# Top-k attention into a Fourier mixing block: the token folds of batches 1 to 6 at one piece a step without a pause, with two fold buffers that change roles for the second parity, and three places for the transposed attention output

## The chip, the core and the metric

The kernel runs on one NeuronCore of a Trainium2 chip. A core has five engines that each work through their own list of instructions in order: TensorE (PE in the profile, with its weight loads as PEld), VectorE (DVE), ScalarE (ACT), GpSimd (POOL) and SyncE (SP, which here only issues DMA transfers). They meet at semaphores. The metric is the device time of one execution in microseconds (us).[...]

## The reference: what is computed

The inputs are q, k and v of shape (8, 8, 576, 64): 8 batches, 8 heads, 576 tokens, 64 channels, and two weights of shapes (512, 2048) and (2048, 512). Everything is float32.

```python
scores = scale * np.matmul(q, k.transpose(0, 1, 3, 2))
kth = np.partition(scores, -32, axis=-1)[..., -32:-31]
scores = np.where(scores >= kth, scores, -1e9)
attn = softmax(scores)                       # over the keys
x = (attn @ v).transpose(0, 2, 1, 3).reshape(8, 576, 512)
mixed = np.real(np.fft.fft(np.fft.fft(x, axis=1), axis=2))
u = x + mixed
un = (u - mean(u)) / sqrt(var(u) + 1e-6)     # over the 512 channels
out = u + np.maximum(un @ w_ch1, 0) @ w_ch2
```

(`softmax` stands for the lines that subtract the largest score, take the exponential and divide by the sum.) The attention of a batch must be complete, for all heads and tokens, before its Fourier part can begin, since that part sums over tokens and over channels.

## The kernel before, in words

**Steps and items.** Two heads make a pair, and a batch has four pairs. A pair's 576 query rows are worked through as nine items: four blocks of 128 rows for each of two heads, and one item that holds the last rows of both. That gives 288 items, 36 to a batch. The program is written by one loop over steps `i`; in each it emits, for all engines, the scores of item `i + 3` (TensorE, lines 368 and 398), the top-32 search of item `i` (VectorE, four MAX8 and three MATCH_REPLACE8 of 576 columns, lines 422 and 424), the threshold `nt` (GpSimd, line 431), mask and exponential of the items just before (ScalarE 445 and 456, GpSimd 448), and the transposition of the probabilities, on TensorE (lines 524 to 539) or, for most pairs, by DMA through a table in DRAM (`planes`, lines 482 and 503). `attend` (line 561) multiplies the probabilities by v, for a pair in two chunks of query columns. `attended` copies the result to a tile `xT` (line 575), and `to_tokens` later transposes it (line 601), multiplies by the reciprocal sums and writes `x`, the batch's 576 by 512 tile. A list `pending` says which chunks are between the two; a chunk of batch b is held there while batch b - 2 has not been stored, as there are two `x` tiles.

**The Fourier part.** The transform over tokens uses symmetry. `fold_ops` makes, for each parity of the frequency (`par` 0 and 1), four pieces: `first` adds or subtracts the two halves of the tokens (`sd`, line 716), `second` adds and subtracts the two halves of the channels (`zw`, line 675), `both` and the last piece fold the channels further (`fg`, lines 648 to 671). For batches 1 to 6 GpSimd does this. `dft_tokens` (line 752) then multiplies `fg` by a table on TensorE, `dft_channels` (lines 809 and 813) does the transform over channels, the result is copied (ScalarE 830), added to `x` (GpSimd 836), normalised by statistics on VectorE (`stats`, lines 841 and 842; `rsqrt`) and transposed (`channels_first`, lines 878 and 881).

**The buffers of the fold.** `sd` takes the buffer `fold_s`, `zw` takes `fold_d`, and `fg` takes `fold_s` again. Both parities use them the same way, so that the second parity's `sd` may only be written when TensorE has read the first parity's `fg`. The two buffers also hold other things at other times, among them the tail's fold, the copy `us`, the transposed `unT` and the MLP's sums `ct`.

**The plan.** Work around the top-k stream is put at fixed steps by `at(step, place, function, cost)`. Batch b's last item is `end`, and its Fourier part begins at `T0`, which is `end + 3` for batch 1, `end + 5` for batches 2 to 6 and `end + 4` for the last. `ft` holds the steps of the two `dft_tokens`, `fc` the first step of `dft_channels`. `arrivals` holds the step at which a batch's MLP is handed to a queue.

**The queue.** The MLP of a batch is cut into units of TensorE work: `hidden` (line 963) and the products of the second layer (lines 990, 1029 and 1160; the latter are the seven products of a scheme with fewer multiplications). A unit has a cost in microseconds written beside it. At each arrival `level` chooses the smallest even load a step, up to about 6.4, at which the queue is empty by the next arrival, and `some` takes units out of the queue between the step's fixed TensorE work until the load is reached. Units that are not done by then stay in the queue ahead of the next batch's. After the last item there is no more top-k work, and TensorE does what is in the queue, then the last batch's Fourier part and MLP. The weights of the seven products are brought from DRAM by `bring` (line 906), on SyncE's queue.

Of the kernel before, what the change touches and what calls it, by code (L numbers as in the profile page):

```python
# [9 lines left out]
F32 = mybir.dt.float32  # L10
# [9 lines left out]
P = 128  # L20
# [53 lines left out]
def kernel(  # L74
# [9 lines left out]
    nc = tc.nc  # L84
    B, H, S, D = q.shape
# [17 lines left out]
    CW = (2 * P + TAIL, 2 * P)  # L103
# [11 lines left out]
    attp = ctx.enter_context(tc.tile_pool(name="attp", bufs=2))  # L115
# [454 lines left out]
    def attended(pair, ch, late):  # L570

        o, w = o_of.pop((pair, ch)), CW[ch]
        PT.pop((pair, ch))
        xT = attp.tile([P, CW[0]], F32, name=f"xT_{pair}_{ch}", tag="xT", bufs=4)
        nc.scalar.copy(out=xT[:, 0:w], in_=o[:, 0:w])
        xT_of[pair, ch] = xT
        den = den_t[pair % 3]
        if ch == 0:
            for h in range(2):
                nc.scalar.copy(  # L580
                    out=den[TH * h:TH * (h + 1), 5:6],
                    in_=den[TAIL + TH * h:TAIL + TH * (h + 1), 4:5],
                )
        c0, n = (0, 6) if ch == 0 else (6, 4)
        rd = small.tile([P, 6], F32, name=f"rd_{pair}_{ch}", tag="rd", bufs=6)

        nc.scalar.activation(out=rd[:, 0:n], in_=den[:, c0:c0 + n], func=AF.Copy, bias=1e-9)
        late.append(lambda: nc.vector.reciprocal(out=rd[:, 0:n], in_=rd[:, 0:n]))
        rd_of[pair, ch] = rd
# [83 lines left out]
    def fold_halves(eng, s_, z):  # L673
        for cols, op in ((slice(0, Q2), ALU.add), (slice(Q2, DM), ALU.subtract)):
            eng.tensor_tensor(out=z[..., cols], in0=s_[..., 0:Q2], in1=s_[..., Q2:DM], op=op)
# [20 lines left out]
    def fold_ops(b, par, eng, space="own"):  # L696

        x = x_of[b]  # L700

        if space == "hT":
            sp = batp.tile([P, NIT * CW[0]], F32, name=f"fsp_{b}", tag="hT")

        def buf(n, name, cols=DM):
            if space == "hT":
                return sp[:, 2 * DM * n:2 * DM * n + 2 * cols].rearrange("p (s c) -> p s c", s=2)
            pool, tag = (batp, ("fold_s", "fold_d")) if space == "own" else (attp, ("PT0", "PT1"))
            return pool.tile([P, 2, cols], F32, name=f"{name}_{b}_{par}", tag=tag[n % 2], bufs=1)

        got = folded[b, par] = []

        def first():
            got.append(buf(0, "sd"))
            op = ALU.add if par == 0 else ALU.subtract
            eng.tensor_tensor(out=got[0], in0=x[:, 0:2, :], in1=x[:, 2:4, :], op=op)

        def second():
            got.append(buf(1, "zw"))
            fold_halves(eng, got[0], got[1])  # L720

        def third(n):
            if n == 0:
                got.append(buf(2, "fg", DM + Q2))
            fold_channels(eng, got[1], got[2][:, :, 0:DM], got[2][:, :, DM:DM + Q2], n)

        def both():
            third(0)
            third(1)

        return [first, second, both, lambda: third(2)]
# [565 lines left out]
    def at(step, where, fn, cost=0.0):  # L1297
        plan.setdefault((step, where), []).append(fn)
        costs[step] = costs.get(step, 0.0) + cost
# [75 lines left out]
    for b in range(B):  # L1375
        end = PER_BATCH * (b + 1) - 1
        last = b == B - 1
        first, soon = b == 0, b == 1
        T0 = end + (2 if first else 3 if soon else 4 if last else 5)
        if first:  # L1380

            for op in fold_tails(b, nc.gpsimd):
                at(T0 - 1, "pool", op)

            def folds(b=b):
                for par, space in ((0, "own"), (1, "hT")):
                    for op in fold_ops(b, par, nc.vector, space):
                        op()
            at(T0, "dve", folds)
            ft, fc = (T0 + 1, T0 + 1), T0 + 1  # L1390
        elif soon:

            for n, op in enumerate(fold_tails(b, nc.gpsimd)):
                at(T0 - 2 + n, "pool0", op)
            for par in range(2):
                def folds(par=par, b=b, T0=T0):
                    for n, op in enumerate(fold_ops(b, par, nc.gpsimd)):
                        at(T0 + 1 + 3 * par + min(n, 2), "pool0", op)
                at(T0, "begin", folds)
            ft, fc = (T0 + 4, T0 + 7), T0 + 8  # L1400
        elif not last:
            for n, op in enumerate(fold_tails(b, nc.gpsimd)):
                at(T0 - 2 + n, "pool0", op)
            for par in range(2):
                def folds(par=par, b=b, T0=T0):
                    for n, op in enumerate(fold_ops(b, par, nc.gpsimd)):
                        at(T0 + (6 if par else 1) + n, "pool0", op)
                at(T0, "begin", folds)
            ft, fc = (T0 + 5, T0 + 11), T0 + 12
        else:  # L1410
            for op in fold_tails(b, nc.gpsimd):
                at(T0 - 1, "pool0", op)

            def folds(b=b):
                for op in fold_ops(b, 0, nc.vector) + fold_ops(b, 1, nc.vector, "PT"):
                    op()
            at(T0, "dve", folds)

            at(T0 + 1, "pe1", lambda: one_unit() + one_unit() if len(queue) > 1 else 0.0)
            ft, fc = (T0 + 1, T0 + 3), T0 + 4  # L1420
        for par in range(2):
            at(ft[par], "pe1", lambda b=b, par=par: dft_tokens(b, par), 4.3)
        for n, t in enumerate((0, 1, 4, 2, 3)):
            quick = first or last
            s = fc + (0 if first else n // 3 if last else n // 2)
            at(s, "pe2", lambda b=b, t=t, q=quick: dft_channels(b, t, q), 1.75)
            if not quick:
                at(s, "pool2", lambda b=b, t=t: add_mixed(b, t))
                at(s + 1, "dve", lambda b=b, t=t: stats(b, t))
            at(s + (1 if quick else 2), "pe", lambda b=b, t=t: channels_first(b, t), 0.6)  # L1430
            if first and t == 4:
                at(s + 1, "pe", lambda: (queue.extend(waiting), waiting.clear()) and 0.0)
        at(s + 1, "begin" if quick else "dve", lambda b=b: rsqrt(b))
        arrivals.append(s + (1 if quick else 2))
        at(arrivals[-1], "units", lambda b=b: (queue if b else waiting).extend(mlp_units(b)))
# [51 lines left out]
    while i < N + 5 or plan or queue or sums:  # L1487
# [26 lines left out]
        if pending and pending[0][0] <= i and (  # L1514
            i < 2 * PER_BATCH + 4 or chunk_at(i)[0] is None
        ):
            _, pp, pc = pending[0]
# [12 lines left out]
        if short:  # L1530
            fixed += tok
            pair, r = divmod(i - 1, PER_PAIR)
# [39 lines left out]
        pair, ch = chunk_at(i)  # L1572
# [78 lines left out]
```

## Time and profile before

| | |
|---|---|
| median of three runs | 1882.73 us (1879.72 to 1884.17) |
| the profiled execution | 1882.96 us, of which the profile spans 1881.2 us |
| TensorE (PE) busy | 1713.1 us, 91% of the span |
| VectorE (DVE) busy | 1582.7 us, 84% |
| ScalarE (ACT) busy | 1295.7 us, 69% |
| GpSimd (POOL) busy | 911.3 us, 48% |
| mean granted TensorE clock | 0.955 of full speed |

How to read it: an engine's busy time is the sum over its instructions in one profiled execution. Busy shares are means over stages that have different limits, so that the stages have to be looked at one by one. A wait is put down to the instruction whose semaphore came last. The duration of a matmul is partly modelled, as matmuls are pipelined. In what follows "step i" in the trace is the moment at which GpSimd begins the threshold `nt` (line 431) of item i: step 39 is at 262.2 us, 88 at 541.6, 126 at 745.9, 162 at 954.9, 198 at 1167.6, 234 at 1370.7, 270 at 1575.9, and the last item, 287, at 1688.1.

### The profile page before, as it was taken

To read this page: it belongs to the slowest core of one execution; us is meant where nothing else is said; L and a number is where in the kernel's file an instruction comes from. 1 tells how busy PE (TensorE), PEld (TensorE's weight loads), DVE (VectorE), ACT (ScalarE), POOL (GpSimd) and SP (SyncE) were. 2 spreads that over 40 slices of the span, in tenths; PEclk is the share of its full clock that TensorE was granted. 3 is DMA by queue.
4 is the path that set the end of the run, shared out by engine and by line. 5 is a ranking of instruction groups with operands and counts; after the bars stand their busy time and mean duration, and the time that the engine had idled before them with its cause. 6 is when DMAs were issued, how large, how long until landed. Compare 5 with 4: busy or idle time off the path is not lost.

```text
span 1881.2 us, 26922 instructions
## 1 busy us (share of the span) xinstructions
PE 1713.1 (91%) x8134; PEld 1086.5 (58%) x8134; DVE 1582.7 (84%) x3301; ACT 1295.7 (69%) x3104; POOL 911.3 (48%) x1278
## 2 busy tenths in 40 slices
PE   5567699889899998989999999999999999999999
PEld 3344364364466654666456665666556655666677
DVE  7999999798899999998899998999999999862110
ACT  6878658576788778777777677777787678652100
POOL 4768643455645356354544465355544465341012
PEclk8887899899899999999999999999999999999999
DMA  5333026651468755585455854685466756440132
GB/s 167 105 96 109 24 60 171 175 138 51 118 155 212 178 125 129 149 214 131 123 144 151 215 128 121 141 229 147 125 155 180 179 133 143 121 117 6 51 110 72
DMA packets 516576, 249.16 MB, mean 132 GB/s; under 512 B 398288, under 2 KB 506448, under 8 KB 516432
## 3 DMA queue, kind: packets, MB, share of 16 engines
q1 hardware_dynamic: 515664, 247.23, 50.7%
q8 instruction: 65, 1.06, 0.2%
q14 instruction: 79, 0.65, 0.1%
q10 hardware_dynamic: 768, 0.21, 0.0%
HBM read 93.63 MB, written 84.74 MB: 95 GB/s over the span
## 4 chain that ended last, share of the span: by engine, by line
PE 66%; ACT 10%; DVE 9%; POOL 7%; issue 3%; DMA 3%; SPq 2%; POOLq 0%; DVEq 0%; ACTq 0%
PE hp L963 24%; PE cp L990 8%; PE o L561 7%; PE sp L398 5%; DVE m L422 4%; PE cw L1160 4%; DVE wk L424 4%; PE yp L752 3%; PE cv L1160 3%; PE cp L1029 3%; POOL wk L448 2%; ACT wk L469 2%; ACT wk L445 2%; PE sp_t L368 2%; ACT S L456 1%
## 5 line engine op out<-in xcount | busy, mean ns | idle before, releaser
L448 POOL TENSOR_TENSOR wk<-S,wk 128x576 f32<-128x576 f32 x288 | 406.7, 1412 | 532.5 <-ACT wk L445 509.8
L422 DVE MAX8 m<-wk 128x8 f32<-128x576 f32 x864 | 626.5, 749 | 6.1
L963 PE MATMUL hp<-unT,w 128*128 128x256 f32 (+1 forms) x2048 | 535.3, 412 | 3.8 <-ACT hT L967 2.6
L963 PEld LDWEIGHTS hp<-unT,w 128*128 128x128 f32 x2048 | 379.4, 192 | 134.5 <-issue 33.4
L424 DVE MATCH_REPLACE8 wk<-m,wk 128x576 f32<-128x576 f32 x576 | 427.4, 742 | 0.0
L469 ACT COPY wk<-S 128x576 uint16<-128x576 uint16 x468 | 288.7, 666 | 0.0
L445 ACT ACTIVATE wk<-S,nt 128x576 f32<-128x576 f32 x288 | 222.5, 773 | 92.6 <-POOL nt L431 91.8
L422 DVE MAX8 m<-S 128x8 f32<-128x576 f32 x288 | 213.9, 743 | 45.1 <-ACT S L372 45.1
L990 PE MATMUL cp<-w,hT 128*128 128x512 f32 x512 | 244.0, 613 | 0.0
L561 PE MATMUL o<-PT,v 128*64 128x256 f32 (+3 forms) x1440 | 203.9, 427 | 21.8 <-DMA PT<-planes 9.9
L967 ACT ACTIVATE hT<-hp 128x320 f32<-128x320 f32 (+1 forms) x256 | 103.4, 408 | 160.2 <-PE hp L963 159.2
L424 DVE MATCH_REPLACE8 wk<-m,S 128x576 f32<-128x576 f32 x288 | 213.5, 741 | 0.0
L456 ACT ACTIVATE S<-wk,nt 128x576 f32<-128x576 f32 x234 | 182.4, 780 | 38.3 <-POOL wk L448 37.3
L398 PE MATMUL sp<-kT,qT 64*128 64x512 f32 (+1 forms) x528 | 181.5, 684 | 12.2 <-ACT means L1348 5.1
L561 PEld LDWEIGHTS o<-PT,v 128*64 128x64 f32 x1440 | 117.0, 157 | 105.7 <-issue 33.8
L401 ACT COPY S<-sp 128x512 f32<-128x512 f32 (+1 forms) x264 | 141.5, 586 | 29.5 <-PE sp L398 28.2
L990 PEld LDWEIGHTS cp<-w,hT 128*128 128x128 f32 x512 | 92.9, 194 | 107.8 <-issue 106.0
L1105 POOL TENSOR_TENSOR hT<-hT 128x512 f32<-128x512 f32 x64 | 81.3, 1274 | 105.1 <-ACT hT L967 91.2
L431 POOL TENSOR_TENSOR nt<-m,cc 128x2 f32<-128x2 f32 x288 | 59.2, 206 | 140.3 <-DVE m L422 139.3
L368 PE MATMUL sp_t<-kt,qT 128*128 128x128 f32 x320 | 70.5, 303 | 43.3 <-ACT S L390 24.4
L368 PEld LDWEIGHTS sp_t<-kt,qT 128*128 128x128 f32 x320 | 55.2, 195 | 92.3 <-ACT S L390 32.4
L1160 PE MATMUL cw<-w,hT 128*128 128x256 f32 x448 | 105.9, 383 | 0.5 <-issue 0.4
(160 smaller groups left out, 2133.1 us busy)
## 6 DMA issues: line engine op xcount, KB each, us to landing
planes<-wk SPq DMA_DIRECT2D x208, 288.0 KB, 2.7
w<-w_parts SPq DMA_DIRECT2D x82, 512.0 KB, 4.7
space<-in_moe_w_ch_dram SPq DMA_DIRECT2D x32, 512.0 KB, 3.7
nat<-in_q_dram SPq DMA_DIRECT2D x128, 64.0 KB, 2.4
v<-in_v_dram SPq DMA_DIRECT2D x64, 128.0 KB, 2.9
out_dram<-x SPq DMA_DIRECT2D x32, 256.0 KB, 2.6
nat<-in_k_dram SPq DMA_DIRECT2D x62, 128.0 KB, 2.9
planes<-wk SPq DMA_DIRECT2D x52, 144.0 KB, 2.7
```

Source lines behind the costliest of these rows:

```text
L368: nc.tensor.matmul(sp[:, 0:P], lhsT=qT[:, q_end - P:q_end], rhs=kt_t, start=True, stop=True)
L398: nc.tensor.matmul(sp[r], lhsT=qT[hd, q_cols], rhs=kT[hd, :], start=True, stop=True)
L422: ops.append(lambda src=src, m8=m8: nc.vector.max(out=m8, in_=src))
L424: ops.append(lambda src=src, m8=m8: nc.vector.match_replace(w, m8, src, NEG))
L445: nc.scalar.activation(out=w, in_=Ssb[i], func=AF.Relu, scale=-FAR, bias=Nt[i][:, 1:2])
L448: nc.gpsimd.tensor_tensor(out=w, in0=Ssb[i], in1=w, op=ALU.subtract)
L456: nc.scalar.activation(out=Ssb[i] if by_dma(i) else w, in_=w, func=AF.Exp, bias=Nt.pop(i)[:, 0:1], accum_out=den_t[pair % 3][:, c:c + 1],)
L469: nc.scalar.copy(out=words[:, half, :], in_=src[:, half, :])
L561: nc.tensor.matmul(o[D * e:D * (e + 1), c0:c1], lhsT=vv[:, c, e, :], rhs=pt[:, NF if c == NF else (NF + 1) * e + c, c0:c1], start=(c == 0) ...
L963: nc.tensor.matmul(hp[:, 0:w], lhsT=w1[:, dt, P * it:P * (it + 1)], rhs=unT[:, dt, 0:w], start=(dt == 0), stop=(dt == NDT - 1),)
L990: nc.tensor.matmul(cp, lhsT=hT[:, it, P * n:P * (n + 1)], rhs=w2[:, it, :], start=(it == 0), stop=(it == NIT - 1),)
L1160: nc.tensor.matmul(dst, lhsT=h()[a][:, kc, :], rhs=rhs_of(kc), start=start and kc == 0, stop=kc == NK - 1, skip_group_check=True,)
```

## The change

Three things are altered.

- The rule for batch 1 and the rule for batches 2 to 6 become one. The four pieces of the first parity stand at steps `T0 + 1` to `T0 + 4`, those of the second at `T0 + 5` to `T0 + 8`, one a step. `dft_tokens` stands at `T0 + 5` and `T0 + 9`, and `dft_channels` begins at `T0 + 10`. Before, batch 1 had two pieces in one step, with `fc` at `T0 + 8`; batches 2 to 6 had a step without a piece between the parities, with `fc` at `T0 + 12`.
- For batches 1 to 6 the second parity uses the two fold buffers the other way round: `sd` in `fold_d`, `zw` in `fold_s`, `fg` in `fold_d`.
- `xT` has three places instead of four.

```diff
-        xT = attp.tile([P, CW[0]], F32, name=f"xT_{pair}_{ch}", tag="xT", bufs=4)
+        xT = attp.tile([P, CW[0]], F32, name=f"xT_{pair}_{ch}", tag="xT", bufs=3)
...
             pool, tag = (batp, ("fold_s", "fold_d")) if space == "own" else (attp, ("PT0", "PT1"))
-            return pool.tile([P, 2, cols], F32, name=f"{name}_{b}_{par}", tag=tag[n % 2], bufs=1)
+            turn_round = par if space == "own" and 0 < b < B - 1 else 0
+            return pool.tile(
+                [P, 2, cols], F32, name=f"{name}_{b}_{par}", tag=tag[(n + turn_round) % 2], bufs=1
+            )
...
-        elif soon:
+        elif not last:
 
             for n, op in enumerate(fold_tails(b, nc.gpsimd)):
                 at(T0 - 2 + n, "pool0", op)
             for par in range(2):
                 def folds(par=par, b=b, T0=T0):
                     for n, op in enumerate(fold_ops(b, par, nc.gpsimd)):
-                        at(T0 + 1 + 3 * par + min(n, 2), "pool0", op)
+                        at(T0 + 1 + (4 if par else 0) + n, "pool0", op)
                 at(T0, "begin", folds)
-            ft, fc = (T0 + 4, T0 + 7), T0 + 8
-        elif not last:
-            for n, op in enumerate(fold_tails(b, nc.gpsimd)):
-                at(T0 - 2 + n, "pool0", op)
-            for par in range(2):
-                def folds(par=par, b=b, T0=T0):
-                    for n, op in enumerate(fold_ops(b, par, nc.gpsimd)):
-                        at(T0 + (6 if par else 1) + n, "pool0", op)
-                at(T0, "begin", folds)
-            ft, fc = (T0 + 5, T0 + 11), T0 + 12
+            ft, fc = (T0 + 5, T0 + 9), T0 + 10
```

Since `arrivals` and `level` are computed from `fc`, the hand-over of the MLP moves too: from steps 39, 86, 128, 164, 200, 236, 272, 297 to steps 39, 88, 126, 162, 198, 234, 270, 297.

## The prediction

> **What bounds the kernel now.** First the 40 slices: TensorE is at nine tenths from the second quarter on, with a lower granted clock at the start.
>
> ```profile
> PE   5567699889899998989999999999999999999999
> PEclk8887899899899999999999999999999999999999
> ```
>
> Then the stages between hand-overs of the MLP (columns: window, length, busy us of PE, PEld, DVE, ACT, POOL, clock, DMA share, GB/s).
>
> ```profile
> core 0: us, PE busy (x) PEld busy (x) DVE busy (x) ACT busy (x) POOL busy (x), PEclk, DMA share, GB/s
> 541.60:745.90 204.30, 191.39 (x922) 116.80 (x921) 196.62 (x404) 160.45 (x383) 104.07 (x144) 0.98 0.64 159
> 745.90:954.90 209.00, 198.34 (x954) 124.98 (x954) 191.07 (x398) 158.21 (x376) 104.73 (x155) 0.98 0.62 155
> 954.90:1167.60 212.70, 204.66 (x966) 128.50 (x965) 191.46 (x399) 158.08 (x376) 104.77 (x156) 0.97 0.60 152
> 1167.60:1370.70 203.10, 196.94 (x962) 124.64 (x961) 191.30 (x399) 157.54 (x376) 104.73 (x155) 0.98 0.63 159
> 1370.70:1575.90 205.20, 198.88 (x964) 125.81 (x963) 192.04 (x399) 157.39 (x375) 104.79 (x155) 0.98 0.64 158
> 1575.90:1688.10 112.20, 110.33 (x527) 72.59 (x526) 93.93 (x197) 70.98 (x169) 44.88 (x65) 1.00 0.50 134
> 1688.10:1881.20 193.10, 188.81 (x856) 141.00 (x854) 28.06 (x69) 31.32 (x78) 30.82 (x52) 1.00 0.17 58
> 262.20:541.60 279.40, 247.09 (x1097) 141.79 (x1096) 254.12 (x520) 207.19 (x520) 146.58 (x212) 0.95 0.50 131
> ```
>
> TensorE idles 32 us in steps 39 to 88 (last row), 13 in steps 88 to 126 (first row), 6 to 11 in each later batch, and hardly in the last two stages. Only the first row has VectorE ahead of TensorE (196.6 against 191.4). So work moved out of the last stage shortens it one for one; in rows 2 to 5 it lengthens the stage; in row 1 some of it fits.
>
> The chain's end shows what fills the last stage. After the last chunk's transposes (1713.4 us) TensorE still does products of batch 6 between the last batch's transforms:
>
> ```profile
> 1713.79 8.59 PE cp L990 x20
> 1722.38 4.15 PE yp L752 x42
> 1726.53 5.15 PE cp L990 x12
> 1731.68 4.17 PE yp L752 x42
> 1749.16 10.30 PE cp L990 x24
> 1759.47 34.45 PE hp L963 x128
> ```
>
> With two groups of four, at 1738.6 and 1746.3 in the timeline, these are 64 records of 0.43 us.
>
> The chain through batch 1's fold shows GpSimd setting the pace there:
>
> ```profile
> 489.12 0.16 POOL nt L431
> ...
> 491.70 3.01 POOL fg L648 x6
> ...
> 494.88 1.35 POOL fg L648 x2
> ...
> 496.49 0.15 POOL nt L431
> ```
>
> Two pieces stand before one threshold, and thresholds are 7.37 us apart. Last, TensorE's waits: the scores' back-pressure, and DMA.
>
> ```profile
> PE sp_t L368 <- ACT S L390: 24.4, 16, 3.6
> PE o L561 <- DMA PT<-planes: 9.9, 4, 7.5
> PE cp L1029 <- DMA w<-w_parts: 5.6, 2, 5.3
> ```
>
> **What the skill says.** The Trainium skill, "Perfetto Trace Analysis" (Engine Utilization and its head), holds matmul busy time for a bad metric since matmuls are pipelined; so I use it for idle time, and compare work by counts of records. "TensorE: Matmul & The Clock Gate" (Part 1) says that an idle window of about 3.4 us lets the clock fall to half. The trace agrees in kind: clock 0.95 in the stage with most idle time, 1.00 in the dense last ones. The same page (Architectural detail) has ACT, DVE and GpSimd as strict FIFOs, which is why `nt` waits behind fold pieces. "GPSIMD Engine Reference" (Instruction dispatch) gives about 2.5 cycles an element for two inputs; at its 1.2 GHz, 1024 elements are an estimated 2.1 us, where the trace has 2.37 for `sd`.
>
> **The change part by part.** The sum is made against the profiled execution, 1882.96 us (span 1881.2), 0.2 above the median.
>
> *Last stage.* The emitted order of the changed kernel has only 12 matmuls of batch 6 (24 records) after the last transposes: two steps more of load before the end let the queue run dry. 40 records fewer by 0.43 is -17.2 us. New exposure: the second parity's fold on VectorE takes 5.1 us after the first, against 4.2 of `yp` and 1.7 of products before it, so it stays hidden; but `hp` must now wait for the copies of `unT`, about 0.5 us each, which products covered, and the channel transform for its copies: +1.5. Sum -15.5.
>
> *Where the 17.2 us go.* Adding the costs that the program itself writes beside its units and fixed work, both plans have the same total, and the changed one has 11 less in steps 39 to 88 (batch 1's transform is two steps later), 15 more in 88 to 126, 3.5 more in 126 to 162, 2 more in 198 to 234, 8 more in 270 to 288. These are amounts of work; a unit of 1.75 is 4 records, 1.72 us measured.
>
> *Steps 39 to 88.* The stage is 32 us idle on TensorE and about 25 on VectorE, partly from a 7.5 us DMA wait that no plan alters; I credit 3 of the 11. The fold: a piece costs `sd` 2.37; `zw` 2 x 1.27 = 2.5; `both` 2 x 0.73 + 4 x 0.46 + small ones = 3.8; the last 2 x 0.73 + 2 x 0.19 = 1.8. With mask subtraction (1.41) and `nt` (0.21), `both` and last in one step are 7.2 us of GpSimd, more than a step's 5.5. Spread, the worst is 5.4. Thresholds 470.58 to 496.49 in that chain are four steps in 25.9 us; at 5.5 they would be 22: -4. Sum -7.
>
> *Steps 88 to 126.* TensorE 191.4 + 15.4 = 207, at the denser stages' clock rather 205; with the later stages' idle time (6 to 8) 212 in place of 204.3: +8. VectorE's 196.6 no longer decides.
>
> *Steps 126 to 270.* 830 us now, with 31 idle. +5.3 of work, against fewer late steps: in each of batches 3 to 6 one step with two channel transforms and a chunk (7.7 planned) disappears. +1.
>
> *Steps 270 to 287.* Dense already: +7.
>
> *The remaining edits.* No pause: the second parity's `dft_tokens` comes one step after its last piece, as the first parity's does already; all transforms together waited only 2.8 us on `fg`, in batch 1. 0, bound +3. Turned buffers: `sd` overwrites what GpSimd itself read, no wait; `zw` in `fold_s` waits for the first `yp` at `T0 + 6`, exactly where `sd` waited before; if late, `nt`, then mask and exponential queue behind it on POOL, up to 1.5 us as once now. `us` comes two steps after its buffer is free. 0. `xT`: before, chunks piled up to four while the store of batch b - 2 was late; in the new order never more than three, so the copy (0.4 us) meets a free place; without that cover it would wait for one `tpx`, 0.4 us. Moved with the units: the `bring` loads, 82 in all, and the stores, on SP's queue among the `planes` transfers. One batch now has 5.3 us of waiting, as its load was issued behind a `planes` store; each new alignment may cost 0 to 5, or save the 5.3. I take 0.
>
> Sum: -15.5 - 7 + 8 + 1 + 7 = -6.5, that is 1876.4; by the median 1876.
>
> **The rivals.**
> *A wash.* The 11 us put off from steps 39 to 88 buy nothing there, and row 1 pays in full: +6.5 on the sum, 1883. For it: idle time there comes from stalls. Against: the GpSimd chain above.
> *The full gain.* Denser work takes both the idle time and the low clock out of steps 88 to 126, and the 5.3 us wait is lost: -8 further, 1868. For it: the last stages show clock 1.00.
> *Slower, by an empty queue.* The new plan empties the queue four to five steps before each hand-over. In its last three steps before that, TensorE has 13 us of planned work while VectorE has three searches (4.9 each: a batch's 191 less some 14 of other work, by 36) plus five `stats` (0.85 each) and `rsqrt`, 19.5. Before, 15.5 stood against the same VectorE work, with 3 to 6 us of idle time around it. If TensorE had no lag to catch up there, it would lose up to 2.7 more in each of five batches, followed by steps too full for VectorE to keep pace; with one lost load alignment of 5 a batch, or both in part, 1891. It decides from 2.1 us a batch. For it: TensorE's waits on the scores' copies fall there. Against: after a dense stretch it does lag, and VectorE idles 12 to 20 us a batch.
> *The change does nothing:* if the second parity's `zw` waited longer than the pause did, hand-overs would not move; the emitted order says that they do.
>
> **How the numbers follow.** Likeliest 0.45, wash 0.22, full gain 0.10, slower 0.23. About 0.2% (3.8 us) is what a measurement can tell from no change: 1879 to 1886.5. Faster: 0.88 of the likeliest, the full gain, 0.12 of the wash: 0.52. Same: 0.12, 0.68 and 0.08 of likeliest, wash and slower: 0.22. Slower 0.26. The likeliest's own range is 1870 to 1881; 8 in 10 reach from the full gain's 1867 to 1890, short of the slower case's far half.
>
> **What would show it.** Last stage: 24 records of `cp` after the last transposes, and from there to the end about 152 us instead of 168. The last transposes come about 10 us later than 1713.4; from 15.7 later on the gain is gone. Batch 1's thresholds during its fold never over 6 us apart. Steps 88 to 126 about 212 us, with TensorE idle 6 to 8. It is wrong if steps 39 to 88 don't shrink, if the five batches after them grow over 2 us each, by idle time before hand-overs or by new waits on `w_parts`, or if `yp` waits on `fg`.

## The result, and the profile after

The changed kernel takes 1911.83 us (median of four runs, 1909.78 to 1915.89); the kernel before took 1883.45 us beside it. The ratio is 1.0153, with a 95% interval of 1.0128 to 1.0178. The change makes the kernel slower by 1.5%; forecast were 1876 us and a range of 1867 to 1890. The profiled execution took 1909.78 us, of which the profile spans 1908.0.

The 40 slices of the changed kernel do not show the loss by eye:

```profile
PE   5666698888899998999899999999889999999999
PEclk8878899999999999999999999999999999999999
```

The stages do. These are all eight, in the columns and the order of the table before (window, length, busy us of PE, PEld, DVE, ACT and POOL, clock, DMA share, GB/s): steps 88 to 126, the four batches from 126 to 270, 270 to 287, the last stage, and 39 to 88.

```profile
core 0: us, PE busy (x) PEld busy (x) DVE busy (x) ACT busy (x) POOL busy (x), PEclk, DMA share, GB/s
539.30:760.00 220.70, 207.88 (x1020) 130.71 (x1019) 201.80 (x419) 166.50 (x397) 107.79 (x161) 0.99 0.63 160
760.00:972.90 212.90, 197.41 (x944) 124.07 (x943) 191.14 (x397) 157.80 (x374) 104.55 (x157) 0.98 0.59 151
972.90:1189.00 216.10, 204.25 (x962) 127.53 (x961) 192.15 (x400) 158.84 (x375) 104.52 (x157) 0.96 0.59 150
1189.00:1408.50 219.50, 205.53 (x989) 128.70 (x988) 192.60 (x400) 158.59 (x376) 104.58 (x157) 0.98 0.59 150
1408.50:1623.30 214.80, 202.22 (x967) 127.59 (x966) 192.03 (x399) 158.11 (x376) 104.62 (x157) 0.98 0.60 151
1623.30:1731.80 108.50, 107.89 (x523) 75.33 (x523) 86.94 (x180) 69.13 (x167) 40.08 (x48) 1.00 0.46 116
1731.80:1908.00 176.20, 171.46 (x776) 125.82 (x774) 27.95 (x69) 27.60 (x68) 30.81 (x52) 1.00 0.19 64
262.60:539.30 276.70, 239.23 (x1060) 135.22 (x1059) 254.15 (x521) 205.08 (x515) 145.98 (x212) 0.93 0.51 129
```

Set against the rows of before, with TensorE's idle time as the length less its busy time:

| steps | before, us | after, us | change | forecast | TensorE idle before | after |
|---|---|---|---|---|---|---|
| 39 to 88 | 279.4 | 276.7 | -2.7 | -7 | 32.3 | 37.5 |
| 88 to 126 | 204.3 | 220.7 | +16.4 | +8 | 12.9 | 12.8 |
| 126 to 270 (four batches) | 830.0 | 863.3 | +33.3 | +1 | 31.2 | 53.9 |
| 270 to 287 | 112.2 | 108.5 | -3.7 | +7 | 1.9 | 0.6 |
| 287 to the end | 193.1 | 176.2 | -16.9 | -15.5 | 4.3 | 4.7 |

The last stage did what was forecast. The four batches in the middle hold the loss, and two thirds of it (22.7 of 33.3) is TensorE standing still. From step 39 to the end TensorE is busy for 1535.9 us now and was for 1536.4: its busy time is the same, and the whole of the 27 us is idle time.

TensorE's waits in the changed kernel (who waits and for whom: us in total, times, longest):

```profile
PE sp_t L368 <- ACT S L401: 29.2, 14, 6.2
PE sp_t L368 <- ACT S L390: 17.3, 11, 2.9
PE o L561 <- DMA PT<-planes: 13.8, 4, 7.3
PE cp L1032 <- DMA w<-w_parts: 7.6, 4, 2.3
PE cw L1163 <- POOL nt L431: 6.5, 5, 1.9
```

The first row in the kernel before:

```profile
PE sp_t L368 <- ACT S L401: 18.7, 13, 6.1
```

The second was 24.4 us before, and fell. The third was 9.9. The fourth was one wait of 5.3 us (and one of 0.3) and is now one of 1.4 to 2.3 in each of four batches. The last row is new. Within steps 126 to 270, where TensorE idles 22.7 us more, the first row grew by 9.9 us (1.0 to 10.9), the second fell by 4.1, the last went from nothing to 5.9, and the load of the weights grew by 2.3; the rest is in smaller waits. (Line numbers after 712 are three higher than before: the product of tile tails 1029 is now 1032, the addition of a plain product's tile 1019 is 1022, the seven products 1160 are 1163.)

**Where the waits stand.** In each of the batches from step 126 on, TensorE stops at the same places of the batch, but for its end. The steps here are those of the batch from 198:
at step 209 for 1.9 us, as `cw` waits for GpSimd, which makes sums for it (line 1108) around the threshold `nt` that the profile names;
at 212 for 2.0 us, as the tails' product waits for its weights;
at 223 for 2.2 us, as `sp_t` waits for ScalarE's copies of scores (4.1 in the batch from 126);
and at 231 and 232, just before the next hand-over, twice for 2.3 us, as TensorE has caught up with VectorE's copies of `x` (in the batches from 126 and 162 there is one wait instead, of 2.4 us at 160 and 3.2 at 196, and for other operands).

The wait at 223 was foreseen nowhere. This is its cause in the timeline of the changed kernel (start, us, engine, line, operation; in brackets how long the engine had been idle and what released it):

```profile
1337.29 0.69 ACT L1020 ACTIVATE hT<-cp,gi 128x512 f32<-128x512 f32 x1 [2.87 <-PE cp L993]
1338.05 1.27 POOL L1022 TENSOR_TENSOR x<-x,hT 128x512 f32<-128x512 f32 x1 [4.54 <-ACT hT L1020]
...
1340.76 1.71 POOL L648 TENSOR_TENSOR fg<-fg 128x128 f32<-128x128 f32 x4
...
1342.59 0.20 POOL L431 TENSOR_TENSOR nt<-m,cc 128x2 f32<-128x2 f32 x1
1342.82 0.78 ACT L445 ACTIVATE wk<-S,nt 128x576 f32<-128x576 f32 x1 [4.84 <-POOL nt L431]
...
1344.63 1.06 ACT L401 COPY S<-sp 128x512 f32<-128x512 f32 x2
...
1345.26 0.49 PE L368 MATMUL sp_t<-kt,qT 128*128 128x128 f32 x2 [2.20 <-ACT S L401]
```

Read it from the top. GpSimd's list has the addition of an MLP tile (L1022) next. Its operand is a product that TensorE is still making, so GpSimd stands for 4.54 us. Behind it in the list are the fold's piece `both` (from 1339.26 to 1342.6) and then the threshold `nt`. ScalarE's mask waits 4.84 us for `nt`; behind the mask in ScalarE's list are the copies of scores; and TensorE, which had made those scores, waits for their place. A product of TensorE's own comes back to it as a wait of 2.2 us, through two other engines. In the kernel before the same addition was emitted at step 229, six steps later (`T0 + 9` instead of `T0 + 3`), and the only piece behind it was the short last one of the second parity; from its timeline:

```profile
1345.82 1.27 POOL L1019 TENSOR_TENSOR x<-x,hT 128x512 f32<-128x512 f32 x1 [2.40 <-ACT hT L1017]
...
1348.65 0.19 POOL L431 TENSOR_TENSOR nt<-m,cc 128x2 f32<-128x2 f32 x1
```

There GpSimd waits 2.40 us, `nt` follows 2.8 us after the addition instead of 4.5, and TensorE has no wait.

The wait at 212 has a tail of its own. This is the tails' product in the changed kernel's timeline, and then a row of its windows (columns as in the stage table):

```profile
1270.25 2.77 PE L1032 MATMUL cp<-w,hT 128*64 128x512 f32 x6 [2.02 <-DMA w<-w_parts]
...
1271.90:1273.60 1.70, 1.70 (x5) 0.65 (x4) 0.00 (x0) 0.00 (x0) 0.00 (x0) 0.50 0.10 35
```

The seventh product is the last reader of the weights that stand in one quarter of the table. When it is done, that quarter is loaded back (`bring`, in two loads issued from 1265.7 to 1267.4), since the tails' product, next in the queue, reads the whole table. Loads of this line land 4.0 to 5.6 us after their issue in this batch, and only two records of other work stood between. TensorE waits 2.0 us, and then runs at a clock of 0.50.

### The profile page after: what moved, and what is told of

Its sections match the earlier page's. It is cut to its first block, busy times and chain, and to the rows that moved or that the text cites. A ratio compares the mean times of both kernels' runs of the same rounds, so it can differ in the third digit from the quotient of the medians.

```text
span 1908.0 us, 26958 instructions
## 1 busy us (share of the span) xinstructions
PE 1712.6 (90%) x8134; PEld 1086.0 (57%) x8134; DVE 1582.6 (83%) x3301; ACT 1296.9 (68%) x3104; POOL 909.7 (48%) x1278
## 4 chain that ended last, share of the span: by engine, by line
PE 62%; DVE 11%; ACT 9%; POOL 8%; DMA 5%; issue 3%; SPq 2%; POOLq 0%; DVEq 0%; ACTq 0%
PE hp L966 23%; PE cp L993 9%; PE o L561 6%; DVE m L422 5%; PE sp L398 4%; DVE wk L424 4%; PE cw L1163 4%; PE cv L1163 4%; PE yp L755 3%; POOL wk L448 3%; PE cp L1032 3%; ACT wk L469 2%; ACT wk L445 2%; DMA planes<-wk 2%; PE sp_t L368 1%
## 5 line engine op out<-in xcount | busy, mean ns | idle before, releaser
L398 PE MATMUL sp<-kT,qT 64*128 64x512 f32 (+1 forms) x528 | 166.8, 665 | 13.9 <-ACT kT L318 7.3
L368 PE MATMUL sp_t<-kt,qT 128*128 128x128 f32 x320 | 70.7, 304 | 46.8 <-ACT S L401 29.2
```

What stands on the lines that cost most here:

```text
L368: nc.tensor.matmul(sp[:, 0:P], lhsT=qT[:, q_end - P:q_end], rhs=kt_t, start=True, stop=True)
L398: nc.tensor.matmul(sp[r], lhsT=qT[hd, q_cols], rhs=kT[hd, :], start=True, stop=True)
```

## The experiments

Three explanations stood against each other. *Collisions*: handing the MLP over two steps earlier puts its addition among fold pieces and moves its weight loads against the steps, so that single instructions come late. *The empty queue*: the plan now has nothing left for the last four to five steps ahead of each hand-over, and TensorE idles there. *The fold itself*: one piece a step without pause, the turned buffers, or three places for `xT`. No kernel below leaves out any part of the computation. Ratios are to the kernel before, run beside each, with 95% intervals. Times by stage are those of each run's one profiled execution.

### Halves of the change

**Old fold, early hand-over.** The kernel before, with `fc` of batches 2 to 6 two steps earlier and all else as it was.

```diff
-            ft, fc = (T0 + 5, T0 + 11), T0 + 12
+            ft, fc = (T0 + 5, T0 + 10), T0 + 10
```

> The kernel before (pause, buffers not turned, four places for xT), with one edit: for batches 2 to 6 the second dft_tokens and dft_channels both begin at T0 + 10, so that the MLP is handed over two steps earlier, at 126, 162, 198, 234, 270, as in the changed kernel. Theory H (it is the earlier hand-over that costs, because the MLP's products and its last additions then meet other steps of the pairs and of the fold): 1895 to 1908 us, TensorE idle 11 us or more in each of the four stages from 126 to 270, with waits at steps 151, 187, 223, 259 and around 160, 196, 232, 268. Theory P (it is the fold without a pause, the turned buffers or the three places): 1878 to 1886 us.

Measured: 1903.05 us, ratio 1.0094 (1.0063 to 1.0126). The last stage falls to 182.5 us, and steps 126 to 270 take 846.2 us against 830.0. Steps 88 to 126 take 220.4 us, as in the changed kernel, though batch 1's hand-over is where it was; a wait of 7.0 us on `w_parts` stands there, at step 103. More such waits, of 0.8 to 3.2 us, stand at steps 141, 142, 177, 178, 214 and 250, and waits of 2.3 at 190, 226 and 262, where the addition now meets the second parity's `sd`. So the early hand-over alone loses 0.9% of the 1.5% that the whole change loses, without the new fold.

**New fold, late hand-over.** The changed kernel, with the hand-over of batches 2 to 6 back at `T0 + 12` and `level` told to plan for 2 us more than there is, so that its queue empties before the hand-over as well.

```diff
-            ft, fc = (T0 + 5, T0 + 9), T0 + 10
+            ft, fc = (T0 + 5, T0 + 9), T0 + (10 if soon else 12)
...
-        while lev < 6.4 and sum(max(0.0, lev - fixed_cost(s)) for s in steps) < rest:
+        while lev < 6.4 and sum(max(0.0, lev - fixed_cost(s)) for s in steps) < rest + 2.0:
```

> The changed kernel, with dft_channels of batches 2 to 6 at T0 + 12, so that they are handed over at 128, 164, 200, 236, 272 as before; fold without a pause, turned buffers and three places stay. The level aims at 2 us of work more than there is, since otherwise four chunks would wait for three places. H: 1880 to 1892 us. P: 1903 us or more. Theory Q (what costs is that the queue is empty some five steps ahead of each hand-over, which this kernel keeps): 1897 us or more.

Measured: 1902.7 us, 1.0094 (1.0059 to 1.013). Steps 126 to 270 take 846.9 us. The wait on `w_parts` has grown to 3.5, 3.7, 2.7 and 4.2 us in the four batches, and one of 6.4 at step 104 is new. This run did not separate the explanations: it moved the loads to other places too, which a later run (with the loads taken out of the question) puts right.

**Batch 1's hand-over late.** The kernel before, with only batch 1's `fc` two steps later.

```diff
-            ft, fc = (T0 + 4, T0 + 7), T0 + 8
+            ft, fc = (T0 + 4, T0 + 7), T0 + 10
```

> The kernel before, with only batch 1's dft_channels two steps later (T0 + 10), so that its MLP is handed over at 88 instead of 86, as in the changed kernel. If batch 1's later hand-over is a main cause: 1890 us or more, with steps 88 to 126 at 212 us or longer. If not (H): 1880 to 1888 us.

Measured: 1880.73 us, 0.997 (0.9952 to 0.9988). Steps 39 to 88 shorten by 3.0 us, as much as in the changed kernel (2.7), with two pieces of the fold still in one step.

### The addition

**One step later.** The changed kernel; the addition is emitted at the end of GpSimd's work of the next step, when its operand is ready, instead of at once.

```diff
-                        nc.gpsimd.tensor_tensor(out=xt, in0=xt, in1=ct, op=ALU.add)
+                        at(now[0] + 1, "pool", lambda: nc.gpsimd.tensor_tensor(
+                            out=xt, in0=xt, in1=ct, op=ALU.add
+                        ))
```

> The changed kernel, with the addition that ends a tile's plain product (GpSimd, x plus ct, one a batch and two in batch 0) put at the end of the next step instead of into the same step ahead of the fold's piece. If GpSimd's wait for that product is what makes TensorE wait at steps 151, 187, 223 and 259, those waits (2.2 to 4.1 us) go and the time falls by 6 to 12 us, to 1900 to 1906. If the wait is only where another lateness shows, the time stays at 1908 to 1915.

Measured: 1888.83 us, 1.001 (0.9995 to 1.0025). Nothing was removed, and 1.4% came back. The waits at 151, 187, 223 and 259 are gone, and the sum of that row in TensorE's waits halves from 29.2:

```profile
PE sp_t L368 <- ACT S L401: 15.6, 9, 6.5
```

Steps 126 to 270 take 849.0 us, 14 less than in the changed kernel.

**At the end of its own step**, behind `nt` instead of ahead of it.

```diff
-                        nc.gpsimd.tensor_tensor(out=xt, in0=xt, in1=ct, op=ALU.add)
+                        at(now[0], "pool", lambda: nc.gpsimd.tensor_tensor(
+                            out=xt, in0=xt, in1=ct, op=ALU.add
+                        ))
```

> The changed kernel, with the addition that ends a tile's plain product still in its own step, but at the step's end on GpSimd: behind the fold's piece and the threshold nt of that step instead of ahead of them. Theory F (what counts is that nt stands behind the waiting addition and the fold's piece in GpSimd's queue): as with one step later, 1884 to 1894 us, no TensorE wait at 151, 187, 223, 259. If the addition has to leave the step altogether: over 1898 us.

Measured: 1886.83 us, 0.9998 (0.998 to 1.0016); 126 to 270 take 845.2 us. What counts is that `nt` does not stand behind the addition; a step of delay adds nothing.

**The kernel before, with the addition a step later** (the same edit as in the first of these two).

```diff
-                        nc.gpsimd.tensor_tensor(out=xt, in0=xt, in1=ct, op=ALU.add)
+                        at(now[0] + 1, "pool", lambda: nc.gpsimd.tensor_tensor(
+                            out=xt, in0=xt, in1=ct, op=ALU.add
+                        ))
```

> The kernel before, with that addition at the end of the next step. If F holds, and the addition in the kernel before meets only the short last piece of the second parity (step 229 in batch 5's time), little is gained: 1878 to 1885 us. If the addition costs as much wherever it stands, some 20 us are gained: 1860 to 1868 us; then the changed kernel's loss isn't due to it.

Measured: 1875.57 us, 0.9922 (0.9898 to 0.9947). The kernel before had the collision too, but elsewhere: it gains 7.0 us in steps 39 to 88 and 2.9 in 88 to 126, and loses 0.5 in 126 to 270, where the changed kernel gains 14.3 by the same edit. The edit is worth 0.8% here and 1.4% in the changed kernel. About 0.6% of the loss is therefore the collision that the change made.

**The same edit on the two halves of the change.** First the old fold with the early hand-over, then batch 1's late hand-over.

```diff
-                        nc.gpsimd.tensor_tensor(out=xt, in0=xt, in1=ct, op=ALU.add)
+                        at(now[0] + 1, "pool", lambda: nc.gpsimd.tensor_tensor(
+                            out=xt, in0=xt, in1=ct, op=ALU.add
+                        ))
```

> The kernel before with the early hand-over of the run e1_old_fold_early (1903 us), and the addition at the end of the next step. F: the waits at 190, 226, 262 (2.3 us each, where the addition met the second parity's sd) go and the time falls by 6 us or more, below 1897. If the early hand-over costs by other ways, the loads of w_parts and the last waits before the hand-over: 1898 to 1905 us.

Measured: 1883.58 us, 0.9982 (0.9971 to 0.9994), 1.1% less than without it; the waits at 190, 226 and 262 are gone. This is 0.3% faster than the changed kernel with the same edit (1.001), although it waits longer on `w_parts` (23.6 us in all, against 10.1). The two differ in the fold and its buffers, in `xT` and in batch 1's hand-over; which of these the 0.3% belongs to was not followed.

> The kernel before with batch 1's hand-over two steps later (1881 us, 0.3% faster than before), and the addition at the end of the next step. If the two gains are separate: 2 to 8 us less than that, 1872 to 1879 us; if the addition was in nobody's way in the old order: 1879 to 1883 us.

Measured: 1870.27 us, 0.9901 (0.9866 to 0.9937).

### The weight load

**Changed kernel, addition later, and the seventh product ahead of the third.** The weights that the seventh product lets go are then loaded back while the third is computed, instead of right ahead of the tails' product.

```diff
-                for f in (p2, p1, p5, p4, p6, p3, p7) for part in range(2)
+                for f in (p2, p1, p5, p4, p6, p7, p3) for part in range(2)
```

> The changed kernel with the addition at the end of the next step (as e4_add_later, 1.001 of before), and the seventh product made ahead of the third one, so that the load of w_parts that the tails' product needs starts two units (3.5 us) earlier. If the waits of the tails' product on that load (0.8 to 3.6 us a batch) are a cost of the new alignment: they go and 5 to 12 us are gained, 1876 to 1884 us. If the time is only spent elsewhere: 1885 to 1890 us.

Measured: 1873.51 us, 0.9922 (0.9905 to 0.994). No wait of the tails' product on `w_parts` is left. What is left in each batch is `cw` on `nt` (1.0 to 1.9 us) and the waits just before the hand-over (1.9 to 3.9 each).

**The order alone, in the changed kernel.**

```diff
-                for f in (p2, p1, p5, p4, p6, p3, p7) for part in range(2)
+                for f in (p2, p1, p5, p4, p6, p7, p3) for part in range(2)
```

> The changed kernel (1.015 of before), with the seventh product ahead of the third one and nothing else. If the late addition and the load of w_parts are two separate costs: about 0.9% off, 1.005 to 1.009 of before, with the TensorE waits at 151, 187, 223, 259 still there. If they are one (the load is late because the addition holds the queue up): 1.000 or below, or no gain at all.

Measured: 1899.63 us, 1.0047 (1.0029 to 1.0064), 1.0% less than the changed kernel. The waits of the tails' product on the load are gone. The waits at 151, 187, 223 and 259 are all there, with 4.1 and three times 2.2 us, in this row:

```profile
PE sp_t L368 <- ACT S L401: 25.9, 14, 4.8
```

So the two edits act on separate waits, and their gains nearly add up (1.4% and 1.0% alone, 2.3% together). But little of this edit's gain is idle time: from step 39 on TensorE idles 109.9 us, against 109.5 in the changed kernel, and is busy for 1524.8 instead of 1535.9 with the same matmuls. It works at half clock for 69.7 us of that time, and for 81.9 without the edit.

**The order alone, in the kernel before; and both edits in it.** The diff is the same.

> The kernel before with the seventh product ahead of the third one and nothing else. It waits on that load in one batch (5.3 us), and the later addition and this edit together gave 1.5%, the addition alone 0.8%. If the edits add up: 0.991 to 0.995. If the load is a cost of the changed kernel's alignment above all, 0.996 to 1.000.

Measured: 1876.95 us, 0.9931 (0.9912 to 0.9951).

> The kernel before with both edits, the control for e9_new_add_p7 (the changed kernel with both, 0.992 of before). The kernel before with the later addition alone stood at 0.992 and had one wait on w_parts, of 6.6 us. Expected 0.986 to 0.990. If 0.990 to 0.994: the change itself costs nothing once both collisions are gone; if 0.987 or less: 0.5% of its loss is still unexplained.

Measured: 1864.64 us, 0.9854 (0.9827 to 0.9881). Alone, the order is worth 0.7% in the kernel before, where one load came 5.3 us late (2.2 with the edit), and 1.0% in the changed one. Here too the busy time falls by more (1536.4 to 1530.9 us from step 39 on) than the idle time (82.5 to 78.7).

**Both edits with batch 1's late hand-over.** The diff is that of batch 1 above, together with the two edits.

> The kernel of e8_batch1_late_add (1870 us), with the seventh product made ahead of the third one. It has such waits in batches 1 and 2 only (2.6 and 5.4 us): 2 to 8 us less, 1862 to 1868 us, if a wait of TensorE on that load counts in full; 1869 to 1872 us if not.

Measured: 1862.7 us, 0.9854 (0.9829 to 0.9879): no gain from batch 1's hand-over is left on top of the two edits.

### The empty queue

**The kernel before with the addition later, and a queue that empties early.** `level` is told to plan for 4 us more than there is, so that the last steps before a hand-over find nothing.

```diff
-        while lev < 6.4 and sum(max(0.0, lev - fixed_cost(s)) for s in steps) < rest:
+        while lev < 6.4 and sum(max(0.0, lev - fixed_cost(s)) for s in steps) < rest + 4.0:
```

> The kernel of e6_before_add (1876 us), with a level that aims at 4 us more work than there is. Hand-overs stay where they were before, but the queue is empty for six steps ahead of each one, as in the changed kernel or more, and the last batch's leftover of seven units shrinks by four or so. Theory Q (the empty queue costs 2 us or more a batch): 1880 to 1890 us. If it costs nothing: 1868 to 1876 us, as the leftover goes.

Measured: 1907.85 us, 1.0102 (1.0083 to 1.012), 1.8% more than without the emptying. But waits on `w_parts` of 7.0, 7.2, 3.3, 4.3 and 3.2 us came with it, so this run priced two things at once.

**The late hand-over with the new fold, addition later.** The diff is that of "New fold, late hand-over" with the addition's.

> The kernel of e2_new_fold_late (fold without a pause, turned buffers, hand-overs of batches 2 to 6 as before, queue empty ahead of them; 1903 us), with the addition at the end of the next step. If the fold without a pause costs nothing by itself: within 5 us of e11_before_add_empty less the 4 us that batch 1's later hand-over gave. If the packed pieces cost: 8 us or more above it.

Measured: 1901.43 us, 1.006 (1.0036 to 1.0084), with waits on `w_parts` of 6.8, 2.7, 2.9, 3.1 and 3.9 us. So it too priced two things at once.

**Both again, with the seventh product earlier.** First the kernel before with both edits and 4 us too much planned, then the new fold with the late hand-over and both edits.

```diff
-                for f in (p2, p1, p5, p4, p6, p3, p7) for part in range(2)
+                for f in (p2, p1, p5, p4, p6, p7, p3) for part in range(2)
```

> The kernel of e11_before_add_empty (1.010 of before: queue empty six steps ahead of each hand-over), with the seventh product ahead of the third one. Theory Q, the empty queue costs by itself: 0.998 or more. Theory L, what cost there were the loads of w_parts (3 to 7 us a batch) and the slow clock after them: 0.980 to 0.992.

Measured: 1880.39 us, 0.9955 (0.9932 to 0.9979). The waits on `w_parts` are gone, and the kernel is still 1.0% slower than with the queue planned as before (0.9854). Steps 88 to 126 take 208.7 us instead of 201.8, with waits of 0.8 and 2.1 us ahead of each later hand-over. So planning 4 us too much costs by itself, without the loads. It does not show as TensorE's idle time, though: from step 39 on this is 77.9 us, against 76.4 in the kernel with both edits, and 25.8 against 26.8 in steps 126 to 270. What grew is the busy time (1538.6 against 1529.2 us), with 71.9 us at half clock instead of 58.0; single profiled executions do not settle why.

> The kernel of e12_new_fold_late_add (1.006 of before: fold without a pause, turned buffers, three places, old hand-overs), with the seventh product ahead of the third one. L, and a packed fold that costs nothing: within 0.4% of e15_before_add_p7_empty, and 0.985 to 0.994. If the packed pieces cost by themselves: 0.5% or more above that run.

Measured: 1875.58 us, 0.9917 (0.9894 to 0.9939). With a queue that also empties early, the new fold is not slower than the old one in the run above. So one piece a step, the turned buffers and three places for `xT` show no cost in this pair. The pair is not a clean one: the plan has 2 us too much here and 4 above, and batch 1's hand-over is later here. With the 0.3% that stayed open above, a small cost of the new fold is not ruled out. (Four places for `xT` with the turned buffers were not tried.)

**Changed kernel with both edits, and a queue that lasts longer.** `level` plans for 1 us less than there is, and the queue is empty for two steps ahead of a hand-over instead of four to five.

```diff
-        while lev < 6.4 and sum(max(0.0, lev - fixed_cost(s)) for s in steps) < rest:
+        while lev < 6.4 and sum(max(0.0, lev - fixed_cost(s)) for s in steps) < rest - 1.0:
```

> The kernel of e9_new_add_p7 (changed kernel, both collisions taken away; 0.992 of before), with a level that aims at 1 us of work less than there is, so that the queue is empty for two steps ahead of each hand-over instead of four or five. If the empty queue is what is left of the loss against e14_before_add_p7 (0.985): 0.986 to 0.990. If it isn't: 0.990 to 0.995.

Measured: 1858.29 us, 0.9831 (0.9812 to 0.9849). One constant is worth 0.9%. The stage from step 198 to 234 (columns of the stage table), without this edit and with it:

```profile
1164.40:1377.40 213.00, 204.51 (x996) 129.94 (x995) 192.98 (x401) 159.00 (x377) 104.54 (x156) 0.99 0.61 154
```

```profile
1156.90:1361.30 204.40, 198.39 (x977) 126.41 (x975) 191.49 (x399) 158.59 (x376) 104.65 (x156) 1.00 0.64 160
```

Both the idle time (8.5 to 6.0 us) and the work (204.5 to 198.4) of this stage are less. Over steps 126 to 270 TensorE idles 26.5 us, against 37.6 without this edit and 31.2 in the kernel before; steps 88 to 126 idle 6.1 instead of 12.2. The last stage pays 6.5 us of it back (184.2 instead of 177.7), as more units are carried to the end. This version beats both kernels: 1.7% faster than the kernel before and 3.2% faster than the changed one (0.9831 by 1.0153).

### The ledger

| | kernel before | changed kernel |
|---|---|---|
| as it is | 1 | 1.0153 |
| addition later | 0.9922 | 1.001 |
| seventh product earlier | 0.9931 | 1.0047 |
| both | 0.9854 | 0.9922 |
| both, and the queue lasts longer | not tried | 0.9831 |

Of the 1.53% by which the change loses, some 0.6% is the addition (1.4% less 0.8%) and some 0.35% the load (1.0% less 0.7%). With both gone 0.7% stays (0.9922 against 0.9854), and the edit to the queue takes out 0.9%. The 0.7% shows as idle time: with both edits TensorE idles 90.1 us from step 39 on in the changed kernel and 76.4 in the kernel before, and the edit to the queue brings it to 73.1. That speaks for the empty queue. It is not proof that the empty queue is all of it: the edit to the queue might gain in the kernel before as well, and there the opposite edit cost 1.0% without adding such idle time. The share of the load is what the order of the products is worth, and most of that came as less busy time, not as shorter waits. The three shares are differences of ratios that have intervals of about 0.2% each way, so they are sizes and not exact parts. What stays open is whether the changed kernel's fold has an advantage of its own over the kernel before once the queue is set well in both, as the last edit was not tried in the kernel before; and, the other way round, the 0.3% above.

## Why the prediction was wrong, point by point

**Right: the last stage.** Forecast -15.5 us, measured -16.9. The chain at the end of the changed kernel has 24 records of `cp` after the last transposes, as the prediction said, and then goes through the two transforms:

```profile
1757.17 0.22 PE tpx L601 x2
1757.39 8.59 PE cp L993 x20
1765.97 4.15 PE yp L755 x42
1770.12 1.72 PE cp L993 x4
```

From these transposes to the end it is 150.8 us, forecast 152. The exposure of `hp` to the copies of `unT`, priced at 1.5 with that of the channel transform, came to one wait of 0.5 us; TensorE's idle time in the stage grew by 0.4. This is most of the 1.4 us of difference. The transposes themselves come 43.8 us later than before, where 10 was forecast and 15.7 was named as the point from which the gain is gone.

**Not contradicted: the remaining edits of the fold.** The second parity's transform without a pause, the turned buffers and three places for `xT` were put at 0. The last run with the new fold and the late hand-over shows no cost of theirs, within the limits said there.

**Wrong: "Steps 126 to 270: +1", measured +33.3.** This is the step that failed, and it failed in its premise. It counted amounts of work, found +5.3 us of it, and took the rest of the stage as it was. It did not ask where each instruction that travels with the units lands in its engine's list. GpSimd's addition was not in the working at all; it now stands ahead of `both` and of the threshold, and this cost about 0.6% of the time (14.3 us of these steps come back when it is moved, and none in the kernel before). The units that moved also brought waits of `cw` for GpSimd that were not there before, 5.9 us in these steps, more than the 2.3 by which the waits on the load grew. The Trainium skill, "TensorE: Matmul & The Clock Gate" (Architectural detail), which the prediction cited to say that `nt` waits behind fold pieces, applies just as well to an addition that itself waits: the trace has GpSimd waiting 4.54 us, ScalarE 4.84 behind it and TensorE 2.20 behind that.

**Wrong: "each new alignment may cost 0 to 5, or save the 5.3. I take 0".** The old wait of 5.3 us was lost and four waits of 1.4 to 2.3 came in its place. In time this was worth about 0.35%, some 7 us. There was one wait of 5.3 us to save, and each of the other alignments could only cost, so that 0 for all of them was a low figure and not the middle one.

**Wrong: "Steps 88 to 126: +8", measured +16.4.** The work came as forecast (TensorE busy +16.5, forecast +15.4; the 2 us taken off for a higher clock did not come, with 0.99 after 0.98), but the idle time was to fall from 13 to between 6 and 8 and stayed at 12.8. With the addition moved, the load relieved and the queue lasting longer it does fall, to 6.1, and the stage takes 207.7 us. What was forecast for this stage was possible, but not in this kernel.

**Half right: "Steps 39 to 88: -7", measured -2.7.** The credit of 3 for the work that leaves the stage has the right size, since batch 1's late hand-over alone gives 3.0. But this is in part luck: with the addition moved out of the way, the same late hand-over gives nothing there (273.3 us, against 272.4 with the early one). The 4 us for the fold were not there. Thresholds during the fold do come closer: the gaps of 7.4 us are gone, and the one of 8.2 that is left at its first step is 4.9 in the kernel with both edits. But the stage hardly gets shorter by it: with the addition moved and batch 1's hand-over late in both, it takes 272.5 us with the new fold and 273.3 with the old one. So GpSimd's pace there was a wait that something else took over. The prediction also misread its table here. It says that only steps 88 to 126 have VectorE ahead of TensorE, but its last row, for steps 39 to 88, has 254.1 us of VectorE and 247.1 of TensorE. What stood in this stage was the addition: moving it gives 7.0 us in the kernel before.

**Wrong, with the other sign: "Steps 270 to 287: +7", measured -3.7.** TensorE was busy for 2.4 us less there, where the planned amounts had 8 more. Why stays open. (The planned amounts of 15, 5.5 and 8 us that the prediction lists enter its sum as 15.4, 5.3 and 7 without a reason; each differs by 1 us at most.)

**The rival "slower by an empty queue"** ended on the right side. The mechanism it names is the likeliest reason for what stays when both collisions are gone, about 0.7% or 13 us of the 28. It was priced alone, with at most one lost load alignment in a batch, at 1891. The kernel went past it since two collisions that the prediction had at 0 came on top.

## What to carry to other kernels

When a block of work is moved, list every instruction that moves with it, on every engine, and for each one ask two things: what does it wait for, and what stands behind it in that engine's list. An instruction that will wait belongs behind the ones that others are waiting for; putting it there cost nothing here. When a planner's target is derived from a date that the change moves, look at how long its queue stands empty ahead of that date: here, work for two or three more of these steps gained 0.9%.

## What the runs showed of the hardware that was not expected

Some short waits of TensorE are followed by a slow stretch. After the wait of 2.0 us at step 212 the clock is 0.50 in the window from 1271.90 to 1273.60, and after that of 2.2 us at step 223 it is 0.65 over the 3.4 us from 1345.3. The Trainium skill, "TensorE: Matmul & The Clock Gate" (Part 1) names idle time of about 3.4 us as what lets the clock fall; here 2.0 to 2.2 us came ahead of it, though not after every wait of that length. Between the kernel before and the changed one this did not decide: the granted clock is 0.955 in both. It does belong to the price of a late load. In all four pairs of kernels that differ in the order of the products alone, TensorE's time at half clock from step 39 on is shorter with the seventh product earlier: 64.9 us instead of 75.1, 69.7 instead of 81.9, 52.6 instead of 61.4, and 58.0 instead of 75.1. Each figure is from one execution.
